# A delta-rule recurrence and an MLP in one kernel: a new plan of engine orders, loads, PSUM banks and constant matmuls

## The chip, the cores and the metric

The kernel runs on one core of one Trainium2 chip. The metric is device microseconds of one execution. A core has a matrix engine (PE, with its weight loads shown as PEld), a vector engine (DVE), an activation engine (ACT), a general engine (POOL) and an engine that here only issues transfers (SP). ACT and POOL issue transfers too. Each engine runs its own instructions in a fixed order, and they wait for each other through semaphores.

## What is computed

The reference runs a delta-rule recurrence over 768 steps for 4 x 8 heads of width 48, then an MLP with GELU over the 3072 tokens of 384 values that it gives:

```python
k_n = k / (np.linalg.norm(k, axis=-1, keepdims=True) + 1e-06)
for t in range(S):
    y[:, :, t] = np.einsum('bhd,bhde->bhe', q[:, :, t], state)
    v_old = np.einsum('bhde,bhd->bhe', state, kt)
    state = state + bt[:, :, :, None] * np.einsum('bhd,bhe->bhde', kt, vt - v_old)
...
x = attn_out.transpose(0, 2, 1, 3).reshape(B * S, H * D)
h = x @ w_in
g = 0.5 * h * (1.0 + np.tanh(c * (h + 0.044715 * h * h * h)))
return g @ w_out
```

Inputs and output are f32; the kernel's matmuls are in bf16.

## The kernel before

**Chunks.** The 768 steps are cut into 12 chunks of 64. Within a chunk the recurrence becomes matrix products with the inverse of a 64 x 64 triangular matrix per head; between chunks only the state S (48 x 48 per head) is handed on. The 32 heads are worked as 16 pairs on 128 partitions.

**Steps of a chunk.** `load` fetches k, q and v (SP's queue). `prep` and `prep2` normalise k (square, sum, root, reciprocal, product: the tiles sq, ss, sr, rn, Kn) and transpose it on PE (L698) into KQT; `prepq` casts q for two chunks at a time (Qn) and transposes it (L666). `gram` multiplies k with k and q (G and DT). The 16 x 16 blocks on the diagonal (`own`) are inverted by substitution: for chunk 0 on DVE (`solve8`, L813), for chunks 1, 2 and 3 together on POOL (`blocks_three` and `solve`, lines L794 and L797, which write into a part of the tile gT), for later chunks in pairs on POOL. The result is spread by a product (XW, L850 and L844), a transpose (`back`, L841: TB) and, for pairs, a small transfer within the chip's own memory (TB<-TB). `factors` and `apply` (chunks 0 and 1) or `inverse` (the others) build the rest of the 64 x 64 inverse by products (TT, ET, DI, WB). `state` then makes R (what is left of v), U (the update), the next S, and the chunk's output, which is evicted as x.

**MLP.** `mlp` works by tiles: chunks 0 to 3 are a tile each, the others go two to a tile, eight tiles in all. For tiles from the third on, twelve or fewer small transfers (x<-x) first bring heads into place. Then come groups of x·W matmuls (into 2048 columns), each followed by GELU on ACT into gT, then the W·gT matmuls, the eviction into one of four output buffers (osb, NOSB = 4) and the stores, which ACT issues. An eviction into a buffer waits for the landing of the stores that the buffer had before.

**Weights.** Ten loads on POOL's queue bring w_in (`load_w1`, `load_w1x`) and w_out (`load_w2`), cast to bf16. They are marked as reading the first q load's buffer (WAFT), so they start when the first q has landed, and the second q load, which overwrites that buffer, starts when all ten have landed.

**The plan.** Nothing is scheduled while the kernel is built. `Plan.op` records each step with what it reads and writes, and numbers the steps in the order of their making. The string `ORDER` (from L20) lists all steps in one sequence: a letter for the engine (p PE, v DVE, a ACT, g POOL, s SP) and the number. So `p187` is step 187 on PE. `schedule` (L135) takes each engine's order from it, and `emit` (L166) sets the semaphore waits that reads, writes, buffers and banks ask for. `BANK` has a digit per PSUM tile: its bank, or the first of its two. A word such as `w11.7` is a constant matmul group (`spin`, L418): 11 matmuls of 128 x 512 zeros into bank 7, whose result nobody reads.

The costs in `op(...)` are a planner's estimates and change nothing in what is built.

Of the kernel before, what the change touches and what calls it, by code (L numbers as in the profile page):

```python
# [21 lines left out]
v88 g20 v86 g16 g13 a89 g17 a90 s59 v91 v92 s56 a106 v65 g93 s57 v66 s58 v107 g14 p96 s99 p94 v73 s98 a108 a33 a109 v70  # L22
v67 v47 v74 s61 v110 a120 v97 g111 s60 v37 a95 v121 a32 p155 a34 a122 a123 a27 v124 v38 p112 v156 g125 s144 v10 v39
a100 v40 v41 g78 v68 a101 p102 v69 s143 g75 a113 v157 p103 g21 g82 v158 v159 g76 p267 a104 v42 g84 a105 v268 v160 v71
a128 v161 g72 p182 v162 v163 p179 v164 v165 v166 p126 v167 g22 v168 g269 v169 a25 v129 a30 a183 v170 v44 a130 g273 v171
a180 v172 v173 a131 a28 a127 v174 g270 v132 v175 p271 g133 v176 g585 v184 p134 v177 a135 g80 v178 g83 v185 a186 p272
g77 v181 g81 p187 a191 v274 g79 p189 a188 p192 v275 a23 p307 a190 p194 v8 v193 g276 g277 a195 p206 g278 p200 a308 g279
p196 v309 g280 p198 a197 g35 g281 a199 p201 g282 p210 g283 a202 s150 p203 g284 p207 s149 g285 p204 v208 g286 v205 g287
v45 p211 g288 s116 v212 g289 s118 v213 g290 v209 s119 p218 a253 g291 s117 p219 s115 g292 v254 p220 g293 p310 g294 a221
p215 a222 g295 s265 a311 p241 g296 a383 s114 g214 g297 s266 v384 g298 p239 g299 v216 a385 g300 a386 p235 g301 a240 v387  # L30
g302 v312 g303 g304 v217 g137 p229 a138 v305 p139 a236 g388 p140 s152 v306 a242 s153 p319 v141 a230 s151 a313 s154 v142
g391 p405 p389 s145 v320 p231 s148 a24 a406 v314 p392 s147 a232 v407 g483 a393 s395 p317 p323 v390 s146 p402 a136 p227
a324 v318 s394 g396 a403 p321 a29 p327 a228 v404 p315 a328 v316 p420 g256 a255 p233 v398 a421 v322 p257 s263 g409 a234
v484 p258 s262 s264 g397 p329 a259 p237 v422 s261 s399 p332 a238 v260 p325 s400 p333 p565 v326 a334 p570 s226 p335 a566
p330 a571 p243 v567 a331 g542 v572 a568 v401 a573 p336 v569 p346 a337 v574 p423 p347 a338 a424 v543 p339 p340 a31 a408
p244 v544 v341 s496 g545 v427 a342 v425 s225 a426 p348 p349 v546 v547 p350 g548 p575 v549 a351 p580 v550 v576 p248 g551
a581 v552 a352 v553 v582 g554 g343 v577 a583 p249 g485 v586 a486 g410 a245 s492 p412 a250 s495 p369 a578 v555 v584 g587
s223 a413 p363 v579 p344 a26 a364 p361 v556 g588 v345 g589 p365 g590 a362 g591 v557 p430 a366 p414 a431 p438 g592 s563
v415 p371 g593 s564 g594 a660 p487 v428 s494 v439 g595 p416 a370 s493 g596 a372 p488 g597 s491 v417 a411 s224 g598 p432
v489 g599 p418 v433 a490 g600 p367 g601 v419 p558 g602 v661 a368 g603 p434 v560 p440 p359 a441 g604 v435 a741 g605 p357  # L40
v559 g606 a429 p442 g607 a360 s353 p561 v443 g608 a358 p444 s356 g609 p436 a662 v562 g610 s355 p445 g611 v742 p764 s354
a446 g612 p373 g613 s672 v743 g614 v765 g744 s673 g615 v766 p374 g616 v745 s455 g618 a767 a251 s454 v768 a456 p497 s453
v746 v622 p769 g747 a451 p378 g617 s449 v437 a452 v498 a770 p379 a375 v748 v623 a771 v749 v750 v751 a772 v752 v619 p499
g753 p503 a754 a500 p461 s620 v755 v773 g756 s621 p504 v380 p627 a505 p774 v628 p457 g663 a246 s510 v775 p779 a458 p469
v776 s671 g625 a462 v780 s670 p459 a470 v781 g624 s447 p463 a777 v785 s515 g784 a460 p471 s762 a464 p465 s669 a782 p473
s763 v635 a466 g786 v783 s514 a859 v778 s450 p629 a472 s512 a513 p639 g787 v630 p501 g788 a247 s511 p467 g789 g790 a626
s668 v637 p664 a468 g791 v860 s448 p665 g792 a382 p474 g793 v502 a638 g794 a640 g795 p478 v759 a666 v636 v475 g796 p631
g797 v667 a477 p647 g798 p641 v632 a252 g799 p479 v648 a934 g800 g801 a381 v642 g802 p633 g803 a480 p643 v634 g804 a861
p653 v935 g805 p649 g806 p524 a650 v644 g807 p516 a481 v936 g808 v937 g1133 a525 p651 p654 a517 v652 p760 a862 p530
g809 v655 g810 a377 p528 g811 a476 g812 p522 v761 g813 a529 g814 p645 a523 g815 g817 p674 a376 v646 p526 v675 a531 g816  # L50
p520 a527 v821 p676 a521 p680 v822 a677 p518 v938 v818 p681 a519 v823 s820 p970 v939 v834 p965 a682 s819 p757 v940 v971
p532 v966 s689 v941 v972 a967 s509 v942 v758 a973 p533 s508 a968 g824 v974 s692 v969 g943 p826 s688 g835 a534 p960 a687
p955 s690 v961 p537 g975 a956 v827 s691 a957 s506 v962 a825 g836 p838 s507 v976 a963 p538 a839 p705 a958 v964 g977 a539
p840 a535 v959 p828 s657 a706 v841 p707 g978 s656 a837 g979 v829 p713 s659 g980 g981 p703 s658 g982 v944 g983 p697 v945
a704 g984 v946 g985 p678 a698 p830 g986 v679 a947 a714 p842 g987 a541 g988 p711 v843 s686 a708 g989 p863 v831 s683 a712
g990 p864 v948 g991 s685 p846 v952 a865 p832 p701 g992 v847 a866 g993 p717 v833 g994 a702 p699 v949 p848 a700 g995 p695
v849 a718 g996 p953 g997 a696 p950 g998 a954 g999 p850 g1000 p721 v851 a951 g1001 p709 g1002 g1003 a536 p852 g1004 p844
a710 g1005 g1006 p853 a722 g1008 v845 p867 a854 p693 v868 g1007 p719 a694 v1012 p723 a540 v1025 a720 p1118 v1009 p869
a724 p1113 v1119 p715 a870 s1011 g1014 v1120 s1010 p733 a1121 v1013 s684 a716 v1122 a1114 p873 p1017 a1115 p874 v1018
g1015 p734 a1116 a875 v1117 g1027 s857 p1123 a482 v735 p1128 s856 p1019 a1124 p729 s881 v1020 a885 s855 a882 s858 a1129  # L60
p730 a1125 v1130 s884 a883 v1134 p737 a880 a1028 a1126 p738 a1016 v1127 g1135 a1131 v731 p1021 a739 p871 g1136 v1022
p725 g1137 g1138 g1139 v872 g1140 p726 g1141 v1026 g1142 v1132 g1143 p1037 g1144 p1029 v1038 p1023 g1145 a1030 p888
g1146 v1024 p898 g1147 a889 g1148 p1031 a899 g1149 p1039 v1032 a727 p902 g1150 a1040 g1151 p910 g1152 a903 p886 g1153
a911 g1154 p1041 a887 p1033 g1155 v1042 a728 p894 g1156 g1157 p890 v1034 a895 g1158 p900 a732 g1159 g1160 a891 p916
g1161 g1162 p1043 a917 g1163 p1035 g1164 p1044 a901 g1166 v1036 p1050 a1045 p896 v1051 g1165 p892 a897 v1170 p1052 a893
p1056 v1053 p914 p906 v1171 v1167 p912 a907 s1169 g1172 a740 p1057 p1175 s1168 v1058 a913 p908 a915 s1046 p904 a909
v1184 s1049 p922 a1061 s1064 a905 v1173 s1060 v1183 a1174 p926 s1059 a1062 g1185 v1176 a1063 s876 a1186 p923 s1047 a736
s878 s879 p1177 a924 p1054 s1048 p927 v1055 s877 p1071 v928 p930 v1178 a1072 p1187 p1179 a1188 p918 v1180 p1195 p1181
v1196 p919 v1182 p1189 a920 p1197 v1190 p1077 a1198 p1085 p1191 a1086 p1199 v1192 a1078 p1089 p931 v1200 a1090 a929
p1204 v932 p1193 p1079 v1194 p1065 v1205 p1075 p1081 a1076 p1083 a1066 a1082 p1208 p1206 a1080 p1067 a1207 p1201 a1068  # L70
p1209 p1202 v1210 p1073 p1069 v1203 p1091 a1070 p1093 a1084 s1215 a1074 p1087 s1214 a1092 p1095 s1216 a1211 p1097 a1213
a925 a1096 p1101 a1212 a933 p1109 a1088 a921 a1094 p1105 p1227 p1235 a1228 p1110 p1217 p1221 a1218 p1098 a1236 a1111
p1245 p1102 a1246 p1219 v1103 p1106 v1099 p1233 a1107 p1243 p1231 p1229 a1232 p1247 a1234 a1230 p1223 a1222 p1241 a1224
p1225 a1220 a1244 p1237 a1226 p1239 a1112 p1249 a1240 a1248 p1253 a1108 a1238 a1242 p1261 a1100 a1104 p1262 p1254 a1263
p1250 a1255 p1257 v1251 a1252 p1258 a1256 a1264 a1259 a1260
# [1395 lines left out]
```

## Time and profile before

| What | us |
|---|---|
| median of 3 runs | 249.35 (249.33 to 250.9) |
| the profiled execution's own time | 247.69 |
| its span, first to last instruction | 245.9 |
| PE busy | 211.0 |
| DVE busy | 161.1 |
| ACT busy | 149.8 |
| POOL busy | 119.6 |
| mean granted PE clock | 0.916 |

Times of the profile count from the first instruction. In a timeline row the columns are start, duration, engine, line, operation, output<-input, form and count; in brackets stand the idle time of the engine before it and what ended it. "Issue" there means that the engine waited for nothing that the profile shows. In a windows row come the stretch, its length, then busy time of PE, PEld, DVE, ACT and POOL with the number of instructions, the granted PE clock, the share of time that the 16 DMA engines are busy on average (it can pass 1, since packets overlap), and GB/s. In the chain that ended last, a row has start, duration and what the time went to.

### The profile page before, as it was taken

How to read it: one execution, taken by the hardware profiler on the slowest of the kernel's cores; microseconds unless marked ns; L12 is line 12 of the kernel's file. 1: busy time of each engine (PE TensorE's matmuls, PEld its weight loads, DVE VectorE, ACT ScalarE, POOL GpSimd, SP SyncE). 2: the span in 40 equal slices, each digit the busy share in tenths (PEclk: the TensorE clock that was granted, in tenths of full speed). 3: DMA queues.
4: the chain of work that ended last, by engine and by line, in shares of the span. 5: the costliest groups of instructions: out<-in, count | busy, mean ns of one | idle time of the engine just before them, and what ended most of it. 6: DMA issues, size and time to landing. Idle time of an engine off the chain costs nothing.

```text
span 245.9 us, 11203 instructions
## 1 busy us (share of the span) xinstructions
PE 211.0 (86%) x5020; PEld 145.0 (59%) x5041; DVE 161.1 (65%) x317; ACT 149.8 (61%) x291; POOL 119.6 (49%) x234
## 2 busy tenths in 40 slices
PE   7354555879997899996999999999999989999995
PEld 2243444667776676875875676665555655555562
DVE  4787933697997878998499786798576783101000
ACT  2468551799998475963588588756762345622830
POOL 1588968477258844888507886438821000000000
PEclk9855555699999999999899999999999999999999
DMA  7999998999646663483212531330215310300123
GB/s 122 168 171 175 181 161 154 181 185 181 132 84 119 111 128 60 103 152 98 51 33 61 109 64 37 68 63 3 69 47 118 63 35 5 113 0 3 37 91 128
DMA packets 64784, 23.76 MB, mean 97 GB/s; under 512 B 53600, under 2 KB 63840, under 8 KB 64736
## 3 DMA queue, kind: packets, MB, share of 16 engines
q1 hardware_dynamic: 57984, 14.67, 36.3%
q0 software_dynamic: 1056, 3.15, 7.6%
q10 hardware_dynamic: 5696, 5.23, 7.4%
q8 instruction: 39, 0.64, 1.1%
q14 instruction: 9, 0.07, 0.1%
HBM read 20.64 MB, written 4.72 MB: 103 GB/s over the span
## 4 chain that ended last, share of the span: by engine, by line
PE 56%; DMA 15%; DVE 9%; SPq 6%; POOL 4%; issue 4%; ACT 3%; ACTq 1%
PE ps L266 53%; SPq L274 6%; DMA W<-in_moe_w_in_dram 5%; DMA qf<-in_q_dram 5%; DMA out_dram<-osb 3%; PE ps L666 2%; DVE S L250 2%; POOL bM L250 2%; DMA TB<-TB 1%; DVE TT L1153 1%; ACTq L274 1%; POOL W L274 1%; PE ps L698 1%; DVE KQT L255 1%; DVE R L250 1%
## 5 line engine op out<-in xcount | busy, mean ns | idle before, releaser
L259 ACT ACTIVATE gT<-ps 128x512 bf16<-128x512 f32 x96 | 54.0, 599 | 32.6 <-PE ps L266 30.7
L266 PE MATMUL ps<-x,W 128*128 128x256 bf16 (+1 forms) x363 | 68.5, 333 | 4.5 <-issue 2.6
L266 PE MATMUL ps<-W,gT 128*128 128x384 bf16 x384 | 67.0, 326 | 0.0
L266 PEld LDWEIGHTS ps<-x,W 128*128 128x128 bf16 x384 | 40.4, 117 | 20.9 <-DVE R L250 0.9
L266 PEld LDWEIGHTS ps<-W,gT 128*128 128x128 bf16 x384 | 36.3, 98 | 24.3
L255 DVE COPY osb<-ps 128x384 f32<-128x384 f32 x9 | 4.9, 552 | 29.9 <-PE ps L266 29.8
L797 POOL TENSOR_TENSOR Yf<-Yf,tmp 128x28 f32<-128x28 f32 (+6 forms) x56 | 21.2, 378 | 4.3
L794 POOL TENSOR_TENSOR tmp<-Yf 128x28 f32<-128x28 f32 (+6 forms) x56 | 20.7, 370 | 4.3
L1046 POOL TENSOR_TENSOR DI<-TB,mB 128x384 bf16<-128x384 bf16 x12 | 11.1, 929 | 20.0 <-DMA TB<-TB 15.5
L266 PE MATMUL ps<-KQT 48*64 48x128 bf16 (+1 forms) x640 | 13.2, 220 | 8.3 <-ACT KQT L259 7.3
L1153 DVE TENSOR_TENSOR TT<-ps,DI 64x384 bf16<-64x384 f32 (+5 forms) x36 | 15.2, 421 | 4.9 <-PE ps L266 4.6
L259 ACT ACTIVATE osb<-ps 128x384 f32<-128x384 f32 x15 | 7.3, 492 | 17.0 <-PE ps L266 13.4
L753 DVE TENSOR_TENSOR DT<-ps,mD 128x512 bf16<-128x512 f32 x24 | 15.9, 676 | 2.1 <-ACT G L259 2.1
L259 ACT ACTIVATE KQT<-ps 128x1024 bf16<-128x1024 bf16 (+1 forms) x14 | 13.8, 991 | 4.9 <-PE ps L698 2.5
L266 PEld LDWEIGHTS ps<-KQT 48*64 48x64 bf16 (+1 forms) x640 | 9.3, 108 | 11.0 <-ACT KQT L259 8.4
L614 DVE TENSOR_REDUCE ss<-sq 128x16 f32<-128x768 f32 (+1 forms) x13 | 11.4, 882 | 6.3 <-ACT sq L259 3.3
L250 DVE TENSOR_TENSOR S<-ps,S 128x768 bf16<-128x768 f32 x10 | 9.6, 957 | 8.5 <-PE ps L266 8.5
L250 DVE TENSOR_TENSOR TT<-ps,DI 128x768 bf16<-128x768 f32 (+2 forms) x18 | 12.1, 687 | 4.4 <-PE ps L266 4.1
L259 ACT ACTIVATE G<-ps 128x512 bf16<-128x512 f32 x24 | 14.1, 598 | 1.1 <-DVE Tt L745 0.9
L259 ACT ACTIVATE sq<-kf 128x768 f32<-128x768 f32 (+1 forms) x10 | 8.1, 812 | 8.2 <-DMA kf<-in_k_dram 6.5
L698 PE MATMUL ps<-identB,Kn 128*128 128x128 bf16 x96 | 9.0, 250 | 4.1 <-POOL Kn L250 3.1
L250 POOL TENSOR_TENSOR Kn<-kf,rn 128x768 bf16<-128x768 f32 (+1 forms) x7 | 10.2, 1460 | 4.6 <-DVE rn L624 2.4
(153 smaller groups left out, 369.0 us busy)
## 6 DMA issues: line engine op xcount, KB each, us to landing
qf<-in_q_dram SPq DMA_DIRECT2D x24, 192.0 KB, 4.5
kf<-in_k_dram SPq DMA_DIRECT2D x23, 192.0 KB, 5.6
vf<-in_v_dram SPq DMA_DIRECT2D x40, 96.0 KB, 3.6
out_dram<-osb ACTq DMA_DIRECT2D x16, 192.0 KB, 2.0
W<-in_moe_w_out_dram POOLq DMA_DIRECT2D x4, 384.0 KB, 12.0
out_dram<-osb ACTq DMA_DIRECT2D x16, 96.0 KB, 2.8
vf<-in_v_dram SPq DMA_DIRECT2D x4, 192.0 KB, 6.5
W<-in_moe_w_in_dram POOLq DMA_DIRECT2D x4, 192.0 KB, 9.5
```

The source lines that it names most:

```text
L250: return lambda e: e.tensor_tensor(out() if callable(out) else out, a() if callable(a) else a, b() if callable(b) else b, op)
L255: return lambda e: e.tensor_copy(out, a() if callable(a) else a)
L259: return lambda e: e.activation(out, a() if callable(a) else a, func)
L266: ins = t.matmul(out, lhsT, rhs, start=st, stop=sp_, skip_group_check=skip)
L274: return lambda e: e.dma_start(out, a)
L614: fr = lambda e, u=u: e.tensor_reduce(ss[j][:, u], sq[:, u, :], AX.X, ALU.add)
L698: ins = e.transpose(tb()[:, m, :], t[:, 2 * m:2 * m + 2, :].rearrange("p h d -> p (h d)"), identB[:, :])
L753: op(d_ps(512), {"dve": lambda e: e.tensor_tensor(dv, gview(1)(), md, ALU.mult)}, reads=[h] + MD, writes=[dn])
L794: sop(nb * s * w, lambda e, s=s, w=w, tv=tv: e.tensor_tensor(tv, yf[:, :, s:s + 1, 0:s].to_broadcast([128, nb, w, s]), Yv()[:, :, s + 1:16 ...
L797: sop(nb * s * w, lambda e, s=s, tv=tv: e.tensor_tensor(Yv()[:, :, s + 1:16, 0:s], Yv()[:, :, s + 1:16, 0:s], tv, ALU.add), [YN, TN], [YN])
L1046: return e.tensor_tensor(o_.rearrange("q p (b j) -> q p b j", j=16), i_.unsqueeze(2).to_broadcast([128, n_, 3, 16]), mB[:, 16 - 16 * w:64 ...
L1153: ins = e.tensor_tensor(TT[r_][o_, par::2, cols], bank(hk, par)[i_, 0:8 * n].rearrange("q (p t) -> q p t", t=n), DI[r_][o_, par::2, 16 * k ...
```

## The change

`ORDER` and `BANK` are written anew; the steps are the same 1265, with the same functions. What the two lists differ in, as far as the text speaks of it:

- Constant matmuls: one group of 11 before, seven groups of 14, 8, 8, 2, 11, 5 and 4 after. All stand in the part before the first x·W group.
- 78 computing steps change engine, most between ACT and DVE, some to or from POOL. Among them the casts of the first S and its spread copy (216, 217) go from DVE to ACT. 21 small x<-x transfers change between SP and ACT.
- The weight loads: before, steps 78, 75, 82, 76, 84 early and 80, 83, 77, 81, 79 later; after, 76, 84, 82 early, 75, 78, 83 behind the product for chunk 3's k, then 79, 81, 80, and 77 behind the first product of the POOL solve (276).
- Chunk 1's gram eviction on DVE (312) stands earlier, so that of the three DVE steps ahead of chunk 1's spreading (305) none is left right before it.
- Stores and x moves are issued at other places of ACT's and SP's orders. The store 252 of tile 0, for example, stands 2.1 us of PE work ahead of the eviction that needs its buffer in the old list, and 34.3 in the new one; the other store of the same buffer, 251, stands 20.5 and 8.5 ahead. PE work here is the sum of PE's busy time in the profile of before over the PE steps that stand between the two in the list (with half of it for steps that ran at half clock).
- On PE, the steps of the recurrence stand at nearly the same place as before, counted in PE work; what stands between them differs.

One line outside the lists changes: the two steps that expand the blocks into DI also wait for the mask mB, which ACT writes once.

```diff
 ORDER = """
-v0 g11 s50 a51 v9 g12 v48 g18 w11.7 v7 s52 a53 v36 v5 v46 v4 v49 s54 v43 v6 v15 s55 v3 v1 a2 s63 s62 a85 g87 p64 g19
...
-g77 v181 g81 p187 a191 v274 g79 p189 a188 p192 v275 a23 p307 a190 p194 v8 v193 g276 g277 a195 p206 g278 p200 a308 g279
...
-g302 v312 g303 g304 v217 g137 p229 a138 v305 p139 a236 g388 p140 s152 v306 a242 s153 p319 v141 a230 s151 a313 s154 v142
...
-g797 v667 a477 p647 g798 p641 v632 a252 g799 p479 v648 a934 g800 g801 a381 v642 g802 p633 g803 a480 p643 v634 g804 a861
...
+g13 s50 a53 g21 v49 g18 g11 a51 s52 g12 v43 v8 v9 v42 v15 s54 v44 v36 v0 v1 a2 s55 w14.2 s63 s62 a85 g87 v86 g16 v6 g19
+v88 g20 s57 a89 a90 s58 v91 v3 s56 v92 a106 s59 p94 p64 v107 a95 g14 g93 s98 g17 p96 v48 a108 s99 g22 v65 a109 v97 s60
+v4 a120 v10 p155 v5 v7 v110 s61 v66 g111 v37 a32 v156 w8.6 a34 v70 v38 v39 v40 v41 v67 v68 v121 s143 v69 a122 a100 g76
...
+v73 v74 a128 v71 v166 p182 g72 v167 p126 v168 v169 v129 a127 g273 v105 a130 a183 v170 w8.3 a27 a29 a131 v132 v171 v184
+g133 v172 v173 p271 p179 v174 g75 v47 v268 g78 v175 g83 p134 w2.0 g269 a135 v176 a180 v177 g79 p307 p272 a30 a33 a191
+g81 v270 w11.0 v274 g80 v178 v275 a186 v181 g276 g77 v185 a308 p189 a25 g277 v309 p187 a190 g278 p192 p194 g279 a193
+w5.5 v195 g280 a188 g281 g282 p200 p196 p210 g283 v197 s150 g284 p201 s149 g285 p198 a202 p206 g286 p207 g287 w4.0 v208
...
+a383 p231 s265 p239 v384 g304 p319 v305 a385 p235 a386 a26 a232 v387 v391 g137 v306 a230 v313 a138 p139 v314 a240 p140
...
 """
-BANK = ("66230771125345763651043331726576350124760117442067461576760254044455202005136577624452212305265072"
+BANK = ("60527063412431043325467342576746364604203125650037372672070265047456005761634627525353421304604531"
...
                             op({"dve": 0.13 + 0.0125 * n, "pool": 0.9}, {"dve": fd, "pool": fd},
-                               reads=hs[0][1][:1] if par == 0 else hs[0][1][1:], writes=nm(name, y) if par else [name + "e"],
+                               reads=(hs[0][1][:1] if par == 0 else hs[0][1][1:]) + MB, writes=nm(name, y) if par else [name + "e"],
                                free=nm(name, y))
```

More of the change, by code (lines that the diff above doesn't have):

```diff
@@ L36 @@
[L36 to L45, printed above, removed]
@@ L51 @@
[L51 to L60, printed above, removed]
@@ L61 @@
[L61 to L75, printed above, removed]
@@ new lines @@
+g1141 v1024 g1142 p890 a911 g1143 v1030 p898 g1144 a891 g1145 p1031 a899 p1039 g1146 s1049 v1032 p888 a1040 g1147 s878
+g1148 p886 a889 s1046 g1149 p902 s1048 a887 g1150 p894 a728 g1151 g1152 p1033 a895 p1041 g1153 a903 p896 v1042 g1154
+a1028 g1155 p916 a897 v1034 g1156 p900 g1157 a917 g1158 p1043 a901 g1159 p1050 p1044 a732 g1160 v1051 p906 g1161 a736
+g1162 p914 v1045 g1163 a907 g1164 g1166 p1035 a915 p912 v1036 p892 v1165 p1052 v1170 a893 p904 a1053 v1167 p908 v1183
+s1168 a913 v1171 p1056 a905 s1169 p1054 a909 p1057 s1047 v1055 p1175 a1058 p922 v1176 a1064 s1063 p923 v1173 a1060
```

62 lines of the change are left out of this document (44 added, 18 removed).

## The prediction

> **What bounds the kernel now.** I read the page first, then the windows by stage, the chain that ended last, and the timelines of the engines where the chain names a wait.
>
> ```profile
> span 245.9 us, 11203 instructions
> PE 211.0 (86%) x5020; PEld 145.0 (59%) x5041; DVE 161.1 (65%) x317; ACT 149.8 (61%) x291; POOL 119.6 (49%) x234
> ...
> PEclk9855555699999999999899999999999999999999
> ...
> q8 instruction: 39, 0.64, 1.1%
> ```
>
> ```profile
> 0.00:43.00 43.00, 23.60 (x564) 16.62 (x564) 27.94 (x85) 21.88 (x49) 30.39 (x59) 0.62 1.15 162
> 43.00:60.00 17.00, 14.14 (x326) 11.56 (x320) 13.96 (x26) 14.47 (x30) 11.40 (x18) 0.87 1.04 180
> 60.00:116.00 56.00, 50.63 (x1476) 38.77 (x1474) 48.12 (x87) 39.71 (x80) 36.79 (x74) 1.00 0.58 114
> 116.00:208.00 92.00, 87.70 (x2476) 58.31 (x2496) 67.46 (x117) 59.32 (x107) 41.05 (x87) 0.98 0.25 55
> 208.00:245.90 37.90, 34.89 (x191) 19.77 (x192) 3.61 (x5) 14.47 (x28) 0.00 (x0) 1.00 0.18 61
> ```
>
> The columns are PE, PEld, DVE, ACT, POOL busy, granted clock, DMA share, GB/s. Two regimes: up to 43 us the DMA share is 1.15 and PE is idle 19.4 of 43.0 us at a clock of 0.62; after it PE is the bound, idle 2.9 + 5.4 + 4.3 + 3.0 = 15.5 us in the other 203. About 2.9 of that is the end (last eviction and store), so at most some 12.6 us of idle after 43 us can be won, and whatever half clock costs there.
>
> ```profile
> 29.89 13.05 DMA W<-in_moe_w_in_dram
> ...
> 44.31 5.31 DMA qf<-in_q_dram
> ...
> 49.67 1.04 POOL Qn L255
> ...
> 50.76 1.08 PE ps L666 x16
> ...
> 54.94 2.99 PE ps L266 x115
> ```
>
> The first regime ends by transfers: the weights are all in at 42.94, the second q load waits for them (its buffer is marked as read by the weight loads) and lands at 49.62, its cast ends at 50.71.
>
> **The change, part by part.** The sum is made against the profiled execution, 247.69 us (span 245.9 and 1.79 around it), which lies 1.66 below the median of 249.35; the difference found is taken off that median.
>
> *The weight loads (POOL).* The same ten loads, in another order: three early instead of five, and the last one (77) now stands behind the first multiply of the POOL solve instead of ahead of it.
>
> ```profile
> 29.89 0.53 POOL L274 DMA_DIRECT2D W<-in_moe_w_in_dram  x1
> 31.89 0.26 POOL L794 TENSOR_TENSOR gT<-gT 128x42 f32<-128x42 f32 x1 [1.48 <-DVE gT L250]
> ...
> 45.98 0.18 POOL L800 MEMSET gT<- 128x48 f32 x1
> ```
>
> So it is issued at about 32.2 instead of 29.89, 2.3 us later. With the whole 13.05 us of the chain's row behind it, it would land at 45.2: +2.3. But that row is queueing: 162 GB/s moved all through this stage, the same bytes have to move, and a piece put in later finds less ahead of it. I take 0; bounds -1.0 and +2.3. Cover if wrong: none, the q load stands right behind it on SP's queue.
>
> *Constant matmuls.* 52 instead of 11, in seven groups instead of one (14, 8, 8, 2, 11, 5, 4).
>
> ```profile
> 0.00:6.15 6.15, 4.88 (x11) 1.49 (x11) 2.77 (x14) 1.74 (x3) 1.04 (x8) 1.00 0.80 122
> ...
> 44.30:47.70 3.40, 3.27 (x53) 2.39 (x44) 1.55 (x3) 2.35 (x6) 1.49 (x6) 0.52 1.02 234
> ```
>
> Eleven took 4.88 us, 0.444 each, at what I read as half rate (the clock record begins only after them). The 41 more cost 18.2 us at half rate, 9.1 at full, against 19.4 us of idle PE in this stage. All stand before the first x·W matmul (45.08, row below), whose start the weights set. I take 0, covered by the weight transfer; without it up to +5 (a rival). Gains too are kept from the end by that transfer. The clock rose only after a stretch as full as 44.30:47.70 (96% busy).
>
> *Chunk 1's factors.* The solve ends on POOL at 46.16, but its spreading on DVE starts at 49.60, behind the casts of S (0.95) and S3 and a gram eviction:
>
> ```profile
> 47.15 0.95 DVE L255 CAST S<-ps 128x768 bf16<-128x768 f32 x1
> ...
> 48.93 0.63 DVE L1245 CAST osb<-ps 48x192 bf16<-48x192 f32 x2
> 49.60 1.41 DVE L850 TENSOR_TENSOR XW<-gT,btz 128x256 bf16<-128x256 f32 x2
> 51.04 0.65 DVE L841 STREAM_TRANSPOSE TB<-XW 128x256 f32<-128x256 f32 x1
> ...
> 54.15 0.73 DVE L955 TENSOR_SCALAR TT<-TB,mBs 128x128 bf16<-128x128 bf16 x4
> ...
> 54.94 0.43 PE L266 MATMUL ps<-TT,G 64*64 64x48 bf16 x16 [0.26 <-DVE TT L955]
> ```
>
> The change puts both casts on ACT and the gram eviction earlier. By the last W issue moved, the solve ends at 46.7; then 1.4 + 0.65 + two TT steps of 0.73 give about 50.3, so TT,G no longer waits for DVE. On PE it then stands behind the second q's transposes, 50.76 to 51.84 as now, and three short steps (a K transpose, an x·W group and a gram, some 1.5 us): about 53.4 instead of 54.94. By then PE has done one x·W group more than now. I take -1.5; bounds -2.5 and 0 (what is late next is the q load).
>
> *Stops inside a step, by "issue".* Four times PE stops in the middle of one step, where no semaphore is waited for:
>
> ```profile
> 37.87 0.41 PE L266 MATMUL ps<-WB,ET 64*64 64x48 bf16 x8 [3.14 <-issue]
> ...
> 58.41 0.25 PE L266 MATMUL ps<-KQT 48*64 48x128 bf16 x3 [0.48 <-issue]
> ...
> 78.26 0.21 PE L266 MATMUL ps<-S,KQT 48*64 48x48 bf16 x1 [1.52 <-issue]
> ...
> 83.91 0.28 PE L698 MATMUL ps<-identB,Kn 128*128 128x128 bf16 x2 [1.00 <-issue]
> ```
>
> Counted along PE's order (a matmul and its weight load as two) they come at instructions 956, 1724, 2748 and 3004: 768, 1024 and 256 apart. Queue q8 brought 39 pieces, 0.64 MB in all, for 10,061 PE and PEld instructions: 16.4 KB, some 256 instructions, a piece. So I read them as PE running out of code while the DMA engines are full. The PE rows between two such borders sum to 3.83, 2.98 and 4.59 us ahead of the last three stops. In the new order, with 82 instructions more in front, the ten pieces from instruction 1212 on sum to 4.04 to 5.23: the shortest is gone, but 4.59 was once not enough. Of 0.48 + 1.52 + 1.00 I take -1.5; bounds -3.0 and +1. The 3.14 lies under the weight transfer: 0.
>
> [...]
>
> *The late store.* ACT issues one store of tile 0 at 110.24, its buffer is wanted by the next eviction, and ACT holds the eviction of U, for which PE's next steps wait:
>
> ```profile
> 110.24 5.07 DMA out_dram<-osb
> ...
> 116.02 0.63 PE L266 MATMUL ps<-R,TT 64*64 64x48 bf16 x32 [2.10 <-ACT osb L259]
> ...
> 112.40:115.80 3.40, 1.52 (x97) 1.34 (x96) 3.01 (x6) 0.42 (x2) 2.97 (x7) 1.00 0.27 74
> 115.80:119.20 3.40, 3.18 (x44) 2.21 (x44) 0.58 (x1) 2.21 (x4) 2.87 (x9) 0.50 0.16 33
> ...
> DMA to landing us min/median/max: 1.9/2.2/5.1
> ```
>
> In the old order 2.1 us of PE work stand between that store and the eviction; in the new one the nearest of the two stores has 8.5. The stop of 2.10 goes, and with it the half clock of the next stretch, 3.18 / 2 = 1.6. The tightest store is now tile 2's, 1.6 us of PE work ahead of its eviction: against the 2.2 us median that is 0.6 on ACT, off PE's path by my reading. I take -3.5; bounds -3.7 and -2.1.
>
> *x moves.* Old: 1.8 us of PE work between the last move and the tile that reads it, twice; new: 3.8 and 2.8.
>
> ```profile
> 96.31 0.82 PE L266 MATMUL ps<-x,W 128*128 128x256 bf16 x6 [0.15 <-DMA x<-x]
> ...
> 134.87 0.59 PE L266 MATMUL ps<-x,W 128*128 128x512 bf16 x2 [0.40 <-DMA x<-x]
> ```
>
> -0.5, at most -0.55.
>
> *The one line outside the plan.* The DI expansions now also wait for ACT's two copies into mB.
>
> ```profile
> L259 ACT ACTIVATE mB<-mb x2: 250/252/253, 23.9 to 31.3; 64x64 bf16<-64x64 f32 x2
> ...
> 58.84 0.91 POOL L1046 TENSOR_TENSOR DI<-TB,mB 128x384 bf16<-128x384 bf16 x1 [0.18 <-DVE TB L841]
> ```
>
> The copies are done 27 us before the first reader: 0. The moves of 78 computing steps between ACT, DVE and POOL change no total that binds (DVE 65%, ACT 61%).
>
> *New waits.* No row shows them. For each PE step I summed the PE rows between its place and its producer's in the list, less the producer's own duration. Between 10 and 60 us of PE work (about 43 to 103 us) 11 of 94 steps fall short by over 0.3 us in the old list and 24 in the new one; after that 25 and 20. So the middle is tighter. Waits of that kind (0.3 to 0.5 us each) on six to eight of the thirteen give +3.0; bounds +0.5 and +6.
>
> Sum: 0 + 0 - 1.5 - 1.5 - 3.5 - 0.5 + 0 + 3.0 = -4.0: 247.69 becomes 243.7, the median 249.35 becomes **245.35**.
>
> **Rivals.** *The waits move, they do not go* (the change doesn't do what it says): the wider margins hold, but the code stops stay and the tighter middle takes 5 us: -1.5 - 3.5 - 0.5 + 5 = -0.5, 248.85. For it: PE's total is the same and idle after 43 us is already only 7.6%. Against it: the store's stop is one clear row.
>
> *Half clock under the constant matmuls (slower).* The group of 11 stands between the own blocks of chunk 3 and chunk 0's first TT,G.
>
> ```profile
> 29.39 1.02 PE L266 MATMUL ps<-TT,G 64*64 64x48 bf16 x21
> ...
> 45.08 3.33 PE L266 MATMUL ps<-x,W 128*128 128x256 bf16 x18
> ```
>
> If the clock is still half there, it lasts 4.9 us from about 30.3, so to 35.2; from that TT,G to the first x·W took 15.7 us (29.39 to 45.08), and the next two groups add 9 x 0.444 = 4.0: x·W would start at 54.9, 9.8 late. PE's idle of 17.00 - 14.14 = 2.9 us between 43 and 60 absorbs part: +6.9. With the store and x gains and the new waits unchanged (-3.5 - 0.5 + 3.0 = -1.0), and no gain in code stops or factors, 255.3; with the 3.14 stop gone in that stretch 252.1. I put it at 253. It decides from chunk 0's TT,G later than about 34. For it: eleven spins alone never held the clock past 10 us. Against: groups of 8, 2 and 11 with work between them make PE nearly full from some 23 us on.
>
> *Full clock from there on.* [...] As a mechanism here: if the groups keep the clock at 1.00 into the x·W work, the 3.27 us of 44.30:47.70 halve, -1.6 more: 243.7.
>
> **How the numbers follow.** Forecast 245.35, chance 0.47; full clock 243.7, 0.11; waits move, 248.85, 0.26; half clock 253, 0.16. Faster by over 1% (under 246.9, about what a measurement of this kernel can tell from no change) 0.58, within 0.26, slower 0.16. The forecast's own range, from its bounds, is 241.5 to 248; the range given reaches to the moved waits and part of the slow case: 241.5 to 251.5.
>
> **What would show it.** Right: no PE stop over 1 us behind osb and no half-clock stretch near 116; the stops by "issue" between 55 and 90 us under 2 us together; TT,G of chunk 1 before 54; the last weight landing by 44. Wrong: TT,G of chunk 0 after 34, weights after 45, or PE's idle from 60 to 116 us above today's 5.4.

## The result, and the profile after

The changed kernel takes 250.84 us (median of 20 executions, 249.02 to 253.1); the kernel before took 249.17 beside it (20 executions, 246.22 to 252.61). The ratio is 1.0107, interval 1.0073 to 1.0141: slower by about 1%, where 245.35 and "faster" had been forecast. The range given reached to 251.5, but for moved waits and half clock; neither is what the runs found, so that 250.84 lies inside it is luck. Ratios here are taken over the executions within 1.5% of each kernel's fastest, medians over all, so the two can differ by half a per cent. The profiled execution took 252.21 us and shows more of the loss than the medians do: 252.21 - 247.69 = 4.5 us against 1.7.

First the page of the changed kernel, then its windows by stage (the columns are those of the prediction's windows).

```profile
span 250.5 us, 11300 instructions
...
PEclk9995799797999999999999999999999999999999
```

```profile
0.00:43.00 43.00, 30.20 (x610) 16.72 (x610) 28.14 (x84) 21.82 (x51) 27.19 (x52) 0.88 1.11 162
43.00:60.00 17.00, 11.70 (x243) 9.17 (x244) 14.76 (x24) 11.33 (x25) 11.67 (x20) 0.86 0.99 169
60.00:116.00 56.00, 51.15 (x1439) 39.52 (x1438) 47.74 (x89) 40.54 (x77) 32.08 (x63) 0.98 0.59 113
116.00:208.00 92.00, 89.73 (x2433) 57.78 (x2431) 70.73 (x126) 54.20 (x100) 47.00 (x97) 1.00 0.27 57
```

The granted clock up to 43 us rose from 0.62 to 0.88 (experiment 9 ties this to the constant matmuls), and the stage from 116 to 208 us is tighter (idle 2.3 us instead of 4.3). One stage is worse: from 43 to 60 us PE stands idle 17.00 - 11.70 = 5.3 us, before 2.9. The timeline of PE shows where (the brackets give the idle time before the row and what ended it):

```profile
42.98 0.25 PE L266 MATMUL ps<-KQT 48*64 48x128 bf16 x4 [1.06 <-issue]
...
45.10 4.45 PE L266 MATMUL ps<-x,W 128*128 128x256 bf16 x24 [0.84 <-ACT x L259]
...
57.24 0.42 PE L266 MATMUL ps<-KQT 48*64 48x128 bf16 x16 [3.20 <-DVE KQT L255]
57.46 0.44 PE L266 MATMUL ps<-TT,G 64*64 64x48 bf16 x16
...
77.66 0.30 PE L266 MATMUL ps<-WB,G 64*64 64x48 bf16 x13 [0.86 <-issue]
```

The first x·W comes at 45.10, as before. Then a new stop of 3.20 us ends at 57.24: a gram waits for the second q's KQT eviction on DVE. The stop of 2.10 behind osb is gone; stops by issue are still there (0.41, 0.86, 0.84, 0.63 and 0.55 us between 72 and 149 us, of which the fence shows one). Of the signs that the prediction named, one failed: chunk 1's TT,G came at 57.46 and not before 54. The others (stop behind osb, stops by issue, last weight, chunk 0's TT,G, PE's idle from 60 to 116 us) came out as for a right forecast. Why the eviction is late is seen on DVE, first as a group, then instruction by instruction, and on POOL beside it:

```profile
50.26 0.64 DVE L841 STREAM_TRANSPOSE TB<-XW 128x256 f32<-128x256 f32 x1
50.93 5.57 DVE L955 TENSOR_SCALAR TT<-TB,mBs 128x128 bf16<-128x128 bf16 x8
...
50.93 0.25 DVE L955 TENSOR_SCALAR TT<-TB,mBs 128x128 bf16<-128x128 bf16 x1
51.10 1.05 DVE L955 TENSOR_SCALAR TT<-TB,mBs 128x128 bf16<-128x128 bf16 x1
52.07 0.66 DVE L955 TENSOR_SCALAR TT<-TB,mBs 128x128 bf16<-128x128 bf16 x1
52.65 0.66 DVE L955 TENSOR_SCALAR TT<-TB,mBs 128x128 bf16<-128x128 bf16 x1
53.23 1.52 DVE L955 TENSOR_SCALAR TT<-TB,mBs 128x128 bf16<-128x128 bf16 x1
54.67 1.50 DVE L955 TENSOR_SCALAR TT<-TB,mBs 128x128 bf16<-128x128 bf16 x1
...
56.41 0.68 DVE L255 COPY KQT<-ps 128x1024 bf16<-128x1024 bf16 x1
```

```profile
49.87 1.15 POOL L255 CAST Qn<-qf 128x768 bf16<-128x768 f32 x1 [2.33 <-DMA qf<-in_q_dram]
50.99 1.11 POOL L844 TENSOR_TENSOR XW<-gT,nbT 128x512 bf16<-128x512 f32 x1
52.06 1.20 POOL L850 TENSOR_TENSOR XW<-gT,nbT 128x256 bf16<-128x256 f32 x2
53.22 1.48 POOL L250 TENSOR_TENSOR Kn<-kf,rn 128x768 bf16<-128x768 f32 x1
54.66 1.46 POOL L250 TENSOR_TENSOR sq<-kf 128x768 f32<-128x768 f32 x1
```

The reader is to lay the two fences side by side. The TENSOR_SCALARs of 1.05, 0.66, 0.66, 1.52 and 1.50 us end at 52.15, 52.73, 53.31, 54.75 and 56.17; POOL's instructions end at 52.10, 52.68, 53.26, 54.70 and 56.12. (The row of 1.20 on POOL holds two instructions of 0.62, and the first of them ends at 52.68.) Each of these five on DVE ends 0.05 us behind one on POOL: in this stretch one gets through per POOL instruction. In the prediction's row four such instructions took 0.73, and each of them started in a pause of POOL (53.75 to 54.66).

### The profile page after: what moved, and what is told of

Same layout as the page of the kernel before. It is cut to its first block, busy times and chain, and to the rows that moved or that the text cites. A ratio compares the mean times of both kernels' runs of the same rounds, so it can differ in the third digit from the quotient of the medians.

```text
span 250.5 us, 11300 instructions
## 1 busy us (share of the span) xinstructions
PE 222.4 (89%) x5082; PEld 145.7 (58%) x5082; DVE 166.3 (66%) x328; ACT 145.3 (58%) x283; POOL 117.9 (47%) x229
## 4 chain that ended last, share of the span: by engine, by line
PE 65%; DVE 15%; ACT 6%; DMA 6%; SPq 4%; issue 3%; DVEq 0%
PE ps L266 60%; SPq L274 4%; DMA kf<-in_k_dram 2%; DVE TT L1153 2%; DVE TT L955 2%; PE ps L698 2%; DMA x<-x 2%; PE ps L666 2%; DVE ss L614 1%; DMA out_dram<-osb 1%; ACT KQT L259 1%; DVE KQT L255 1%; DVE x L255 1%; DVE DT L753 1%; DVE R L250 1%
## 5 line engine op out<-in xcount | busy, mean ns | idle before, releaser
L266 PE MATMUL ps<-x,W 128*128 128x256 bf16 (+1 forms) x384 | 72.4, 336 | 3.0 <-DMA x<-x 1.5
L259 ACT ACTIVATE osb<-ps 128x384 f32<-128x384 f32 x16 | 7.9, 492 | 28.2 <-PE ps L266 27.6
L797 POOL TENSOR_TENSOR Yf<-Yf,tmp 128x28 f32<-128x28 f32 (+6 forms) x56 | 21.8, 389 | 4.3
L421 PE MATMUL ps<-wz 128*128 128x512 bf16 x52 | 16.3, 468 | 4.4 <-DVE warm L428 3.2
L266 PE MATMUL ps<-KQT 48*64 48x128 bf16 (+1 forms) x640 | 13.4, 214 | 7.2 <-DVE KQT L255 4.6
L1046 POOL TENSOR_TENSOR DI<-TB,mB 128x384 bf16<-128x384 bf16 x13 | 11.8, 928 | 15.6 <-DMA TB<-TB 13.7
L259 ACT ACTIVATE KQT<-ps 128x1024 bf16<-128x1024 bf16 (+1 forms) x13 | 12.9, 990 | 6.2 <-PE ps L698 5.7
L250 DVE TENSOR_TENSOR R<-ps,vf 128x768 bf16<-128x768 f32 x11 | 10.5, 953 | 4.5 <-PE ps L266 4.5
L250 POOL TENSOR_TENSOR Kn<-kf,rn 128x768 bf16<-128x768 f32 (+1 forms) x6 | 8.6, 1437 | 10.0 <-DVE rn L647 5.9
L266 PEld LDWEIGHTS ps<-TT,ET 64*64 64x64 bf16 x640 | 9.8, 109 | 5.8 <-issue 2.4
```

Of the source, the lines that this page charges most:

```text
L250: return lambda e: e.tensor_tensor(out() if callable(out) else out, a() if callable(a) else a, b() if callable(b) else b, op)
L259: return lambda e: e.activation(out, a() if callable(a) else a, func)
L266: ins = t.matmul(out, lhsT, rhs, start=st, stop=sp_, skip_group_check=skip)
L421: ins = e.matmul(psum[:, b, :], wz[:, 0:128], wz[:, :], start=True, stop=True)
L797: sop(nb * s * w, lambda e, s=s, tv=tv: e.tensor_tensor(Yv()[:, :, s + 1:16, 0:s], Yv()[:, :, s + 1:16, 0:s], tv, ALU.add), [YN, TN], [YN])
L1046: return e.tensor_tensor(o_.rearrange("q p (b j) -> q p b j", j=16), i_.unsqueeze(2).to_broadcast([128, n_, 3, 16]), mB[:, 16 - 16 * w:64 ...
```

## The experiments

Numbers of steps are those of the order list. "The kernel before" was run beside each set.

**1. One of the two TT steps back on ACT.**

```diff
-... a230 v313 a138 p139 v314 ...
+... a230 a138 a313 p139 v314 ...
```

> The changed kernel, with the first of chunk 1's two TT steps (313) back on ACT; the second (314) stays on DVE. Theory A (DVE stands still beside POOL: each TENSOR_SCALAR of these steps waits for the end of the POOL instruction in hand, and the 5.57 us of the eight are the main loss): the four that are left take 2.4 us or less from about 50.9, the KQT evictions behind them start by 53.6 instead of 56.41, PE's stop of 3.20 us ahead of 57.24 falls below 0.8, the half clock of 58.8 to 62.2 goes with it (1.7 us), and the time falls by 3 to 5 us against the changed kernel, to 0.990 to 0.999 of the kernel before. Rival B (the loss is taken up anyway by the next wait): the stop goes, but the time stays within 1 us of the changed kernel's, 1.007 to 1.014 of the kernel before.

Measured: 246.45 us (before 248.21), ratio 0.9961, interval 0.9912 to 1.0011. DVE of this kernel:

```profile
50.77 2.97 DVE L955 TENSOR_SCALAR TT<-TB,mBs 128x128 bf16<-128x128 bf16 x4
53.66 0.68 DVE L255 COPY KQT<-ps 128x1024 bf16<-128x1024 bf16 x1
```

The four that are left take 2.97 us in all, more than the 2.4 expected and 0.74 each where four in a pause take 0.18 each, but there are only four; the eviction starts at 53.66, PE's stop of 3.20 is gone (the longest from 50 to 60 us is 1.06, behind ACT), and so is the half clock that followed. Theory A.

**2. The same steps on DVE, POOL held back.**

```diff
-               reads=[YN, "nbT"] + x, writes=["XW0"])
+               reads=[YN, "nbT"] + x + (["TT1b_0", "TT1b_1"] if x else []), writes=["XW0"])
(the same for XW1)
```

> The changed kernel, with one wait added: the two XW spreads on POOL (397, 396), and with them Kn and sq behind them, start only when the two TT steps on DVE are done. Nothing moves to another engine. Theory A (the POOL instruction beside it holds DVE up): the eight TENSOR_SCALAR take 1.3 to 2.0 us instead of 5.57, the KQT evictions start by 53.6, PE's stop of 3.20 falls below 0.8, time 3 to 5 us below the changed kernel, 0.990 to 0.999 of the kernel before. Rival C (these eight are slow by themselves, by their source or by their number): they still take 5 us or more, POOL's work comes 4 us later, and the time is the changed kernel's or up to 2 us longer, 1.007 to 1.020.

Measured: 244.99 us (before 248.21), ratio 0.9917, interval 0.9869 to 0.9964. DVE, then the window from 43 to 60 us:

```profile
51.30 1.40 DVE L955 TENSOR_SCALAR TT<-TB,mBs 128x128 bf16<-128x128 bf16 x8
53.02 0.69 DVE L255 COPY KQT<-ps 128x1024 bf16<-128x1024 bf16 x1 [0.32 <-PE ps L666]
```

```profile
43.00:60.00 17.00, 15.06 (x330) 11.90 (x322) 14.20 (x30) 14.12 (x30) 10.85 (x18) 0.82 0.82 151
```

Nothing left DVE and nothing was taken out; a wait was added. The same eight instructions take 1.40 us instead of 5.57, the KQT eviction now waits for PE and not PE for it, and PE is idle 1.94 us from 43 to 60 instead of 5.3. Rival C falls: the eight are slow only with POOL beside them. The median moved from 1.7 us above the kernel before to 3.2 below: 4.9 us; the two ratios, 1.0107 and 0.9917, are 1.9% or some 4.7 us apart.

**3. Eleven constant matmuls instead of 52 in the changed kernel.**

```diff
-w14.2 ... w8.6 ... w8.3 ... w2.0 ... w11.0 ... w5.5 ... w4.0
+w11.2
```

> The changed kernel with 11 constant matmuls in one group, as before, instead of 52 in seven; everything else as changed. Theory D (they cost and bring nothing: the weights set the first x*W): granted clock up to 43 us back from 0.88 to about 0.62, first x*W still at 45.1 within 0.3, time within 1 us of the changed kernel. Rival E (they pay, by the clock that they keep up): half clock again up to 47.6 and the time 1 to 2 us longer. Rival F (they cost: they push chunk 0's TT,G from 29.4 to 33.6 and crowd what follows): TT,G of chunk 0 before 31, and 1 to 3 us shorter. On the stops by issue: the list of PE's instructions is 82 shorter from the first group on. If they come from code that is not there yet at each 256th instruction, they come at other steps than now (each border some 82 instructions later in the work); if from a wait of the work itself, at the same steps as in the changed kernel (48 x 64 K transposes at 72.1 and 76.8, and so on).

Measured: 251.76 us (before 248.21), ratio 1.0194, interval 1.0139 to 1.025: 3.6 us above the kernel before, where the changed kernel was 1.7 above and, in experiment 10, 3.4. The clock up to 43 us is 0.61 and the first x·W comes only at 47.89, which theory D excluded; F falls too (chunk 0's TT,G came at 35.15, not before 31), and E holds in its direction; its size is 0.2 to 1.9 us in the medians and some 2.2 in the ratios. The stops by issue of 72 to 77 us are at none of their old steps; the profile shows none over 0.4 us after 43 us here, so this run does not test the borders.

**4. The kernel before with its late store alone issued early.**

```diff
-... p629 a472 ... v632 a252 g799 ...
+... p629 a252 a472 ... v632 g799 ...
```

> The kernel before with a single edit: the second store of tile 0's second half (252) is issued by ACT right behind the x*W step 629, some 8 us of PE work ahead of the eviction that wants its buffer, instead of 2.1. Theory G (the prediction's term holds by itself): the stop of 2.10 us at 116 goes and with it the half clock of 115.8 to 119.2, time 3 to 3.7 us below the kernel before, 0.985 to 0.988. Rival H (another store or eviction is late next, or the stop only moves): 0 to 1.5 us, 0.994 to 1.000.

Measured: 247.99 us (before 248.21), ratio 0.9967, interval 0.9914 to 1.0021. There is no stop behind osb at 116, but the 3 to 3.7 us are not found: theory G falls, H holds.

**5. The kernel before once more.**

> The kernel before, unedited, one look at another execution. If its stops are fixed by the program (as the prediction took them): the store at about 110 lands after some 5 us and PE stops 2.1 us at 116 with half clock behind it; stops by issue of 0.48, 1.52 and 1.00 us at PE's instructions 1724, 2748 and 3004. If they are chance: the store lands in about 2.2 us, its median, and the stop at 116 is under 0.5; the stops by issue have other lengths or come at other borders of 256, and the half-clock stretches behind them elsewhere.

Measured: 251.46 us in one execution, 3.8 us more than the one that the prediction was worked from. Its DVE and its PE:

```profile
54.30 2.60 DVE L955 TENSOR_SCALAR TT<-TB,mBs 128x128 bf16<-128x128 bf16 x4
```

```profile
56.96 0.43 PE L266 MATMUL ps<-TT,G 64*64 64x48 bf16 x16 [2.04 <-DVE TT L955]
...
80.44 0.21 PE L266 MATMUL ps<-S,KQT 48*64 48x48 bf16 x1 [1.06 <-issue]
...
99.87 1.44 PE L266 MATMUL ps<-x,W 128*128 128x256 bf16 x6 [2.63 <-DMA x<-x]
```

With the same program as before: no stop over 0.4 us at 116; the stop by issue inside the S,KQT step again; those of 0.48 and 1.00 not; an x move that cost 0.15 the first time costs 2.63; and the four TENSOR_SCALAR of chunk 1 take 2.60 instead of 0.73, because the k load landed earlier (at 54.0 instead of 54.6) and sq ran on POOL from 54.07 to 55.54. So most of these single stops are chance, and one, by the S,KQT step, came again.

**6. The kernel before with step 313 on DVE: one part of the change alone.**

```diff
-... p319 v141 a230 s151 a313 ...
+... p319 v141 a230 s151 v313 ...
```

> The kernel before with one part of the change alone: step 313 (the first of chunk 1's TT steps) on DVE, behind the first KQT eviction, instead of ACT. Theory A (TENSOR_SCALAR waits for the POOL instruction in hand): it meets the two POOL multiplies for Kn (50.7 to 53.8), its first instruction takes about 1.2 us and the four 1.5 to 2.5 instead of 0.7; the second KQT eviction and R come as much later; time 0 to 2 us longer than the kernel before, 1.000 to 1.008, less than in the changed kernel because only one POOL instruction is in the way and not five. Rival C (the eight are slow only in the changed kernel, by something else): 0.7 for the four, 0.997 to 1.003.

Measured: 248.91 us (before 248.87), ratio 1.0026, interval 0.998 to 1.0073. Its DVE and POOL:

```profile
52.68 0.74 DVE L955 TENSOR_SCALAR TT<-TB,mBs 128x128 bf16<-128x128 bf16 x4
...
54.79 1.89 DVE L955 TENSOR_SCALAR TT<-TB,mBs 128x128 bf16<-128x128 bf16 x4
```

```profile
49.42 3.27 POOL L250 TENSOR_TENSOR Kn<-kf,rn 128x768 bf16<-128x768 f32 x2
53.85 1.47 POOL L250 TENSOR_TENSOR sq<-kf 128x768 f32<-128x768 f32 x1 [1.16 <-PE ps L698]
```

The 1.5 to 2.5 us expected for step 313 did not come: its four started at 52.68, when POOL had just ended (49.42 + 3.27 = 52.69) and paused for 1.16 us, and took 0.74. The four of step 314, beside sq, took 1.89. For step 313 the numbers are those of rival C (0.7 us, no change in time), but its four had not met POOL; the four of step 314 did. That is the same hold-up once more inside one kernel (0.74 against 1.89), but no loss in time: the time alone tells nothing here.

**7. Experiment 2 and four constant matmuls ahead of the first x·W.**

```diff
-... a311 p229 ...
+... a311 w4.2 p229 ...
```

> The changed kernel with the added wait of POOL (as in the run before of that kind: XW spreads only behind the TT steps) and one group more of four constant matmuls ahead of the first x*W step, where PE is idle 0.8 us and the granted clock falls to half for 3.4 to 7 us. Theory K (the clock falls because PE is not full there): clock 1.00 through 43 to 50, first x*W at 45.1 to 45.4, 1.5 to 3 us less than without the group: 0.980 to 0.987 of the kernel before. Rival L (it falls by the stop by issue of 1.1 to 1.7 us at 41 to 42.5, which no matmul can fill): half clock as before, time within 0.7 us of the kernel without the group, 0.989 to 0.995.

Measured: 244.85 us (before 248.87), ratio 0.981, interval 0.976 to 0.986, the lowest ratio of all, from six executions. PE and its windows (PE busy and clock among the columns):

```profile
43.67 3.01 PE L266 MATMUL ps<-x,W 128*128 128x256 bf16 x24
...
50.06 1.76 PE L666 MATMUL ps<-identB,Qn 128*128 128x128 bf16 x16 [2.23 <-ACT gT L259]
```

```profile
48.00:50.00 2.00, 0.00 (x0) 1.00 0.98 169
50.00:52.00 2.00, 1.88 (x20) 0.62 0.31 47
52.00:54.00 2.00, 2.00 (x21) 0.52 0.93 244
```

The 24 matmuls of x·W ran at full clock, 3.01 us instead of 4.69 in experiment 2, as theory K has it. Part of the gain need not be the group's: the stop by issue ahead of x·W was 0.43 us here and 1.68 in experiment 2, and x·W started at 43.67 instead of 45.24. PE then stood still for 2.23 us, and the half clock came behind that gap instead.

**8. Experiment 2 with the late store of the kernel before.**

```diff
-... p414 a252 p438 ... a376 p479 ...
+... p414 p438 ... a376 a252 p479 ...
```

> The changed kernel with the added wait of POOL, and the store of the change undone: store 252 is issued right ahead of step 479, some 2 us of PE work before the eviction that wants its buffer, as in the kernel before. Theory G (the late store costs what the profile of before shows, each time): a stop of about 2 us on PE behind osb, half clock behind it, 3 to 3.7 us longer than without this edit, 1.004 to 1.010 of the kernel before. Rival H (that store was late by chance, a landing of 5.1 us against a median of 2.2): no stop over 0.6, 0 to 1 us, 0.990 to 0.997.

Measured: 246.34 us (before 248.87), ratio 0.9867, interval 0.9814 to 0.992. The stop is

```profile
113.42 0.44 PE L266 MATMUL ps<-R,TT 64*64 64x48 bf16 x32 [0.52 <-ACT osb L259]
```

half a microsecond, without half clock behind it: theory G falls here too. With experiment 4: the late store cost 0.52 us here, and 2.10 and the clock in the one execution that the prediction was worked from.

**9. Experiment 2 with eleven constant matmuls.** The edit is that of experiments 2 and 3 together.

> The changed kernel with the added wait of POOL, and only 11 constant matmuls, in one group, as in the kernel before: the worth of the 41 others where the stop behind the TT steps doesn't cover it. Theory M (they pay by the clock): half clock again from 10 to about 47 and the time 1.5 to 2.5 us longer than with them, 0.996 to 1.002 of the kernel before. Theory N (the weights set the first x*W, so they bring nothing, the prediction's term of 0): 0.986 to 0.994, as with them.

Measured: 246.92 us (before 248.39), ratio 1.0036, interval 0.9998 to 1.0074.

```profile
47.68 2.08 PE L266 MATMUL ps<-x,W 128*128 128x256 bf16 x9 [0.84 <-ACT x L259]
```

In the new order the first x·W comes at 47.68 without the 41 constant matmuls and at 45.24 with them (experiment 2), behind the same cast of x on ACT both times, and not behind a transfer; the clock up to 43 us was 0.64 against 0.95. In the medians 244.99 is 3.2 us below the kernel before and 246.92 is 1.5 below: 1.7 us; the ratios, 0.9917 and 1.0036, lie some 3.0 us apart. Theory M, with a loss at or above the upper end of what it had; theory N falls.

**10. The changed kernel once more.**

> The changed kernel, unedited, again. If the loss is fixed by the order: the eight TENSOR_SCALAR take 5 to 6 us once more, PE stops 2.5 to 3.5 us ahead of the gram that needs the KQT eviction, half clock behind it; time 1.007 to 1.015 of the kernel before. If it was chance: under 3 us and 0.990 to 1.003. The stops by issue between 60 and 160 us (3.3 us in the first profile) are expected at other borders or shorter, since they were gone in two kernels with the same PE list.

Measured: 251.75 us, the median of six executions (before 248.39). DVE and PE of its profile:

```profile
49.23 5.56 DVE L955 TENSOR_SCALAR TT<-TB,mBs 128x128 bf16<-128x128 bf16 x8
```

```profile
55.54 0.42 PE L266 MATMUL ps<-KQT 48*64 48x128 bf16 x16 [3.19 <-DVE KQT L255]
```

5.56 for 5.57 and 3.19 for 3.20: this loss is the program's. The half clock behind the stop lasted 6.8 us here, from 56.7. The stops by issue after 43 us were 0.85 and 0.90, 1.75 us against 3.3 in the first profile.

**11. Experiment 7 and eight more constant matmuls ahead of the second q's transposes.**

```diff
-... a311 p229 ... a138 p139 ...
+... a311 w4.2 p229 ... a138 w8.2 p139 ...
```

> The changed kernel with the added wait of POOL, the group of four constant matmuls ahead of the first x*W step, and eight more ahead of the second q's transposes, where PE was idle for 2.2 us and the clock fell to half behind it (50.6 to 53.8). Theory K (the clock falls behind a stretch that PE does not fill): clock 1.00 from 7 us on, 1 to 1.7 us less than with the first group alone, 0.973 to 0.980 of the kernel before. Rival L (the eight hold up the transposes, or the clock falls anyway): 0.980 to 0.988.

Measured: 246.23 us (before 248.39), ratio 0.9996, interval 0.9951 to 1.0041. That is outside what theory K (0.973 to 0.980) and rival L (0.980 to 0.988) had. In the profiled execution the clock fell at 44.05, ahead of both groups, and a stop by issue stands before it:

```profile
42.73 0.25 PE L266 MATMUL ps<-KQT 48*64 48x128 bf16 x4 [2.08 <-issue]
```

The same stop was 0.43 in experiment 7. The gap of 2.23 ahead of the transposes was filled, and no half clock came there. So whether a group ahead of x·W pays is open: 0.981 and 0.9996 stand for nearly the same program, and their difference from experiment 2's 0.9917 is not settled in either direction.

**12. The kernel before with sq on POOL behind step 314.**

```diff
-                   reads=kn, writes=[f"sq{n}"] + ["sq1"] * (len(parts) == 1))
+                   reads=kn + ["TT1b_1"] * (c == 6), writes=[f"sq{n}"] + ["sq1"] * (len(parts) == 1))
```

> The kernel before with one wait added: the sq multiply on POOL that stands at about 54 to 56 us (step 483) starts only behind the TT step 314 on DVE. In four looks with the old order the four TENSOR_SCALAR of 314 took 0.73, 2.16, 2.60 and 1.89 us: 0.73 where they came ahead of sq, more where sq and XW were under way. Theory A (the kernel before draws the same loss by chance): the four take 0.65 to 0.80, PE stops under 0.5 us behind TT, no half clock at 55 to 61, and the median falls by 0.5 to 2 us: 0.992 to 0.998. Rival B (the time is given back at the next wait, or sq comes too late): 0.998 to 1.003.

Measured: 248.0 us (before 248.45), ratio 1.0054, interval 0.9998 to 1.0111. DVE and PE:

```profile
49.52 2.06 DVE L850 TENSOR_TENSOR XW<-gT,btz 128x256 bf16<-128x256 f32 x2
...
54.47 0.73 DVE L955 TENSOR_SCALAR TT<-TB,mBs 128x128 bf16<-128x128 bf16 x4
```

```profile
53.02 0.42 PE L266 MATMUL ps<-KQT 48*64 48x128 bf16 x16 [1.64 <-DVE KQT L255]
...
79.80 0.21 PE L266 MATMUL ps<-S,KQT 48*64 48x48 bf16 x1 [2.05 <-issue]
```

The four take 0.73 as wanted, and no time is won: the gain of theory A did not come and rival B is nearer, though 1.0054 lies above its 1.003. In this execution the pair L850 ahead of them, beside POOL's cast of Qn and Kn (48.83 to 52.88), took 2.06 (0.77 in experiment 5, where POOL stood idle) and made the same kind of stop one step earlier. Whether that alone gave the gain back was not tried.

## Why the prediction was wrong

**Chunk 1's factors (-1.5, bounds -2.5 to 0): the step that failed.** It let the solve's end, 1.41 + 0.65 and two TT steps of 0.73 follow each other, so that "TT,G no longer waits for DVE". The 0.73 came from a row at which POOL paused; in the new order POOL has five multiplies in a row exactly there (50.99 to 56.12), and the change moves step 313 from ACT, where its four took 1.27 us beside POOL's Kn in the profile before (from 51.83), to DVE. Shown by experiments 1, 2 and 10: 5.57 and 5.56 us with POOL beside them, 1.40 with POOL held. The price is in the after trace: 3.20 us of stop on PE, and half clock behind it. In windows,

```profile
58.00:59.00 1.00, 0.82 (x35) 0.91 1.47 158
59.00:60.00 1.00, 1.00 (x25) 0.50 1.48 170
60.00:61.00 1.00, 1.00 (x13) 0.50 1.29 129
61.00:62.00 1.00, 1.00 (x22) 0.50 0.01 1
62.00:63.00 1.00, 1.00 (x37) 0.89 0.16 33
```

that is 0.18 + 3 + 0.22 = 3.4 us at half rate, 1.7 us lost. 3.20 + 1.7 = 4.9, and 4.9 is what experiment 2 won back in the medians. So the term was about +4.9 and not -1.5: 6.4 us, more than the whole miss of 1.7 + 4.0 = 5.7. That the two figures of 4.9 are equal is partly chance: in experiment 10's trace the same sum is 3.19 + 6.8 / 2 = 6.6 (and its six executions against experiment 2 give 3.4 + 3.2 = 6.6), while experiment 2's own trace has more half clock ahead of 50 us than the changed kernel's (0.82 against 0.86 from 43 to 60). The bound of 0 had not priced the neighbour on POOL, and no rival had either. A row of the prediction already showed it: its 1.41 for the spreading L850 is 0.77 in experiment 5 and in the changed kernel; in the profile before, the second of the two ran beside POOL's cast of Qn and took 1.06. The gain itself was not there: with POOL held, chunk 1's TT,G starts at 54.73, not at 53.4, behind a KQT eviction on ACT.

Of the hold-up itself the trace shows this much: one TENSOR_SCALAR per POOL instruction, ending 0.05 us behind it, while the transposition of 0.64 us at 50.26, beside the cast on POOL (49.87 to 51.02), was not held up (the twelve transpositions of this line took 0.60 to 0.65 in this trace). Why POOL holds the one and not the other, no run here shows.

**The late store (-3.5).** The mechanism is real (one eviction on ACT waited 3.6 us for a landing in the profile before), its size was one execution's. Four other profiles of a store that late show 0.47 (experiment 12), 0.52 (experiment 8) and no stop over 0.4 us (experiments 5 and 6); the landing took 2.3 to 3.5 us in them. About -0.5 was there to win. The row that should have warned stood in the prediction: this landing took 5.1 us, the median 2.2.

**Code stops (-1.5).** Counted along PE's order, the stops by issue lie at the same place of each 256 instructions in both kernels and all experiments in which they were counted (by the order list; the loads in the trace give up to some 30 less: in the old order at 1724, 2748, 3004 and, in experiment 5, 6588; in the new one at 1212, 2236, 2492 and, in experiments 1 and 8, 8124). Which of these borders cost anything changes with the execution, with one exception: the one in the S,KQT step of the old order cost 1.52, 1.63, 1.06, 1.23 and 2.05 us in five profiles, while the one at 1212 in the new order cost 0 to 2.08. After 43 us the stops over 0.4 us come to 3.0, 1.6, 1.5, 1.9 and 3.1 us in five profiles of the old order, 2.2 in the mean, and to 3.3, 1.75, 0.8, 0, 0.8, 0.4 and 3.1 in the seven of the new one that keep its constant matmuls, 1.5. So about -0.8: right in sign, half the size, and not to be read from one profile. That the stops are missing code was the author's reading of this spacing and is not shown: no run took code away. That they need full DMA engines, as it had it, is not so: the DMA share in the stops that ended at 78.26 and 83.91 us was 0.41 and 0.46 in the kernel before, and 0.03 and 0.05 in those that ended at 77.66 and 91.20 in the changed one.

**x moves (-0.5) and new waits (+3.0).** An x move cost 0.15 and 2.63 in two executions of the same program; the term is chance too. For the new waits take all idle time of PE after 43 us: 15.5, 10.2, 13.4, 13.1 and 14.6 us in five profiles of the old order, 13.4 in the mean; 8.3, 9.1, 11.2 and 12.9 in the four of the new order with POOL held and the constant matmuls kept, 10.4 (the trace of before has 363 of the 384 x·W matmuls, which makes such sums rough). So store, code stops, x moves and new waits together are worth some -3.0; the prediction had -3.5 - 1.5 - 0.5 + 3.0 = -2.5. The totals hold every other wait of PE as well and no half clock, so this is an estimate. By it the sum of the four about held though neither the store nor the code stops had their size, and that is luck.

**Weights and constant matmuls (0 and 0).** The last weight landed at 42.76 and the first x·W started at 45.10, as forecast. But the cover named for the constant matmuls, the weight transfer, was not what set the start: without them it is 47.68 (experiment 9), and with them 45.24 in experiment 2, where the last weight had landed at 41.30. They pay some 1 to 3 us, by the clock as the windows suggest, and that seems to make good what the new order, without them, would lose ahead of x·W. The slow rival, half clock under them, did not occur: chunk 0's TT,G came at 33.6, under the 34 at which it was to decide.

With the term of the factors set right, the sum is -2.5 + 4.9 = +2.4; measured +1.7. The prediction's "own range, from its bounds" of 241.5 to 248 is not their sum, either: the bounds of its terms add up to -10.2 and +6.7, or some 239 to 256, and it does not say how it got narrower. The kernel of experiment 2 (244.99 against 248.21) beats the kernel before by 0.8%, interval 0.4 to 1.3.

## What to carry to other kernels

When a step moves to DVE, look at what POOL does at the new time: a duration from a row where POOL paused is no price (four took 0.73 there, eight 5.57 beside POOL), and a wait that held POOL back for some 3 us (its XW started at 52.78 and not behind its cast at 49.91) was worth 4.9 here. Price a single stop from more than one execution of the same program, or by the median of its kind; here the stop that looked best to win was mostly chance. And test a cover by taking the covered work away: the constant matmuls cost nothing, but not for the reason given.

## What the runs showed of the hardware

- A TENSOR_SCALAR of 128x128 that took 0.25 us with POOL paused (two in a row 0.41 in the kernel before, eight 1.40 in experiment 2, since they overlap) took 0.66 to 1.52 for the five of eight that ended 0.05 us behind a POOL instruction in the changed kernel; two evictions from PSUM beside POOL's Kn took 1.42 in the kernel before, 0.71 each, and one with POOL idle 0.68 in the changed one. The TENSOR_TENSOR pair of L850 took 0.77 with POOL idle (experiment 5 and the changed kernel) and 1.41, 2.06, 2.18 and 2.37 beside POOL's cast of Qn and Kn (the kernel before, experiments 12, 4 and 6).
- The granted clock fell to half behind gaps on PE of 2.10 us (before), 2.23 (experiment 7) and 3.20 (after), each time for about 3.4 us, starting between 0.2 us ahead of the gap's end and 1.6 us after it; behind the 3.19 of experiment 10 it lasted 6.8. After a stop of 1.42 us in experiment 1 (PE at 109 us, behind ACT) it did not fall. In the changed kernel it also fell at about 45 us (0.58 from 45 to 46, 0.50 from 46 to 48), behind stops of 1.06 and 0.84, so the runs give no one length of gap at which it falls.
- The kernel before spread over 246.2 to 252.6 us in 20 executions. Which stops by issue, x moves and meetings of DVE and POOL an execution draws differs, and the long ones can bring half clock as well, as experiment 5's clock row shows at 56 to 62 us and at 100 to 106 us, behind the stops of 2.04 and 2.63:

```profile
PEclk9855555697999999599999999999999999999999
```
